# Four alternating attention layers on one core: full layers project queries and keys in five unpadded blocks, and most of the last output projection is moved ahead of the last head group

## The chip, the cores and the metric

The kernel runs on one core of a Trainium2 chip. The metric is device time in microseconds (us) from the first to the last instruction's end on that core. "Granted clock" is the share of full TensorE clock that the hardware allowed, as the profile records it.

## The reference, cut to what matters

```python
def _A_ref(x, wqkv, wo):                      # windowed layer; B is the same without the mask
    B, S, D = x.shape                         # 1, 2048, 640
    H = 32; Dh = D // H; W = 256              # 32 heads of 20
    q, k, v = ...                             # x @ wqkv, split by head
    scores = einsum("bhqd,bhkd->bhqk", q, k) * (Dh ** -0.5)
    mask = (idx[:, None] - idx[None, :] >= 0) & (idx[:, None] - idx[None, :] < W)
    p = softmax(where(mask, scores, -1e9))
    return merge_heads(einsum("bhqk,bhkd->bhqd", p, v)) @ wo

x = A_x
x = x + _A_ref(_layernorm(x), A_wqkv, A_wo)   # layer 0, windowed
x = x + _B_ref(_layernorm(x), B_wqkv, B_wo)   # layer 1, full
x = x + _A_ref(_layernorm(x), A_wqkv, A_wo)   # layer 2, windowed
x = x + _B_ref(_layernorm(x), B_wqkv, B_wo)   # layer 3, full
```

All data are bf16. A head has 20 elements.

## The kernel before

The kernel splits the 2048 tokens into 4 chunks of 512 and the 32 heads into 8 groups of 4. A *unit* is one chunk of queries of one group of heads in one layer. Its scores come out transposed (keys on the 128 partitions, 512 queries along the free axis), three banks of PSUM at a time: three score matmuls, one exponential of 128x1536 on ScalarE. This is a *tile*. Two tiles of PSUM alternate. Value matmuls follow two or three tiles later.

The four heads of a group lie in four strips of 32 partitions. A head has 20 elements, and in this kernel the other 12 rows of each strip hold zeros, because the projection weights are padded with zero columns. The score matmul reads the whole strip, 32 rows:

```python
def k(self, kc, j):
    ...
    return t[32 * j : 32 * j + 32, o * P : (o + 1) * P]
def q(self, j, q0, qn):
    ...
    return t[32 * j : 32 * j + 32, q0 * P : (q0 + qn) * P]
```

Full layers project each group of each chunk (eight groups, five matmuls of 512 columns each, for queries and for keys), store the padded result to HBM and load it back one unit at a time:

```python
def t_full(l, n, c, g):                       # n: 0 queries, 1 keys; 8 groups g
    while "prep_b" not in ready: yield ("wait", 1)
    ...
    wt = yield from take_w(l, n, c, g)
    yield from project(wt, xnT[l, c], staged) # five matmuls, then an eviction
    dst = k_d[l][:, g, c * C : (c + 1) * C] if n else q_d[l][:, c, g, :]
    nc.sync.dma_start(out=dst, in_=staging.pop())
```

Projections, values and output projections are generators that a scheduler steps while it emits tiles. A step ("hold", cost) keeps the same task running; a step ("pe", cost) lets another one come next:

```python
def project(wt, xt, dst):
    mb = yield from take_m()
    pq = ps[:, mb, :]
    for dc in range(KD):                      # KD = 5
        nc.tensor.matmul(pq, lhsT=wt[:, dc, :], rhs=xt[:, dc, :],
                         start=(dc == 0), stop=(dc == KD - 1))
        if dc < KD - 1:
            yield ("hold", 0.22)
    evac(dst(), pq)
    drop_m(mb)
    yield ("pe", 0.22)
```

The very last output projection (8 blocks of 128x320, each a sum over 8 head groups) runs when the last head group has been normalised, so all 64 matmuls and 8 additions stand after the last exponential.

The softmax here doesn't subtract the row's maximum and nothing guards it: scores larger than these inputs give would overflow.

## Time and profile before

| | before |
|---|---|
| time, median of 4 fast runs of the comparison | 2517.38 us (2514.48 to 2525.18) |
| profiled execution | 2509.4 us, mean granted clock 0.762 |
| exponentials | 1695, the same in every kernel here |
| projection matmuls of queries and keys | 1280 |
| TensorE busy / ScalarE busy | 81% / 90% |

The prediction shows most lines of this profile. One that it does not show is the granted clock in the 40 equal slices of the span (a digit is tenths of full speed), from the page of the kernel before:

```profile
PEclk9899899887866798958888589769865575557555
```

Read it from left to right: nearly full clock in layer 0, some 0.8 through the long mixed stretch, and about 0.55 in the last quarter, where only full attention is left.

### The profile page before, as it was taken

What the parts mean: (1) busy time and instruction counts of PE and PEld (TensorE: products, weight loads), DVE (VectorE), ACT (ScalarE), POOL (GpSimd) and SP (SyncE); (2) the same over time, 40 slices, a digit from 0 to 9 for tenths busy, and PEclk for the clock granted to TensorE, in tenths of its full rate; (3) what the DMA queues carried; (4) which work ended last, traced back from release to release, by engine and by line L of the source; (5) the groups of instructions that cost most, each with busy time, mean ns of one, the idle gap of its engine ahead of it and who ended that gap; (6) DMA issues with size and microseconds to landing.
All of it is one profiled execution on the core that took longest, in us unless ns stands there. A gap on an engine that the chain in (4) does not pass through costs nothing.

```text
span 2509.4 us, 37786 instructions
## 1 busy us (share of the span) xinstructions
PE 2037.4 (81%) x15424; PEld 729.9 (29%) x15424; DVE 868.8 (35%) x1956; ACT 2251.3 (90%) x1812; POOL 48.4 (2%) x129
## 2 busy tenths in 40 slices
PE   6889798788887888778887889788877777777777
PEld 3344233222322233223322233232222222222222
DVE  6787575222242334343335334542210010001001
ACT  6778687799989998999989988899999999999995
POOL 2000000000000000000000000000000000000000
PEclk9899899887866798958888589769865575557555
DMA  4221322421210123112222034013211010011000
GB/s 156 79 69 50 110 82 80 124 89 64 67 54 17 48 60 117 45 33 59 65 74 71 1 96 123 25 34 93 85 39 48 33 43 33 33 41 51 33 17 11
DMA packets 114637, 153.70 MB, mean 61 GB/s; under 512 B 11296, under 2 KB 97824, under 8 KB 114464
## 3 DMA queue, kind: packets, MB, share of 16 engines
q1 hardware_dynamic: 114464, 151.30, 19.9%
q8 instruction: 120, 1.97, 0.3%
q14 instruction: 53, 0.43, 0.1%
HBM read 121.11 MB, written 30.15 MB: 60 GB/s over the span
## 4 chain that ended last, share of the span: by engine, by line
ACT 44%; PE 30%; issue 15%; DVE 9%; DMA 2%; SPq 0%; POOL 0%; ACTq 0%; DVEq 0%; POOLq 0%
ACT pt L834 43%; PE ps L318 10%; PE ps L820 7%; PE ps L874 4%; PE ps L484 4%; PE ps L405 3%; DVE pt L859 3%; DMA wqk<-wqk_d 1%; DVE st L269 1%; PE ps L369 1%; DVE oT L682 1%; PE ps L728 1%; DVE x_sb L492 1%; DVE qa L269 0%; DVE on L732 0%
## 5 line engine op out<-in xcount | busy, mean ns | idle before, releaser
L834 ACT ACTIVATE pt<-ps 128x1536 bf16<-128x1536 f32 (+2 forms) x1695 | 2196.4, 1513 | 191.7 <-PE ps L820 167.7
L820 PE MATMUL ps<-qt,kt 32*128 32x512 bf16 x4096 | 695.4, 491 | 313.8 <-ACT pt L834 296.4
L874 PE MATMUL ps<-pt,vt 128*21 128x512 bf16 x4096 | 518.4, 493 | 10.9 <-DVE oT L680 4.2
L820 PEld LDWEIGHTS <-kt 32*128 32x128 bf16 x4096 | 202.3, 95 | 761.7 <-issue 744.0
L318 PE MATMUL ps<-xnT,wqk 128*128 128x512 bf16 x1280 | 369.5, 427 | 31.6 <-DMA wqk<-wqk_d 19.4
L859 DVE TENSOR_TENSOR pt<-pt,masks 128x1024 bf16<-128x1024 bf16 (+6 forms) x403 | 239.0, 625 | 148.7 <-ACT pt L834 148.4
L682 DVE CAST oT<-ps 128x512 bf16<-128x512 f32 x112 | 76.7, 685 | 451.1 <-PE ps L874 450.8
L874 PEld LDWEIGHTS <-vt 128*21 128x21 bf16 x4096 | 106.1, 91 | 327.0 <-issue 322.0
L484 PE MATMUL ps<-wop,on 128*128 128x320 bf16 x1024 | 180.3, 325 | 8.9 <-DVE x_sb L492 6.3
L318 PEld LDWEIGHTS <-wqk 128*128 128x128 bf16 x1280 | 118.2, 105 | 211.7 <-issue 110.4
L269 DVE CAST st<-ps 128x512 bf16<-128x512 f32 x124 | 85.7, 691 | 232.6 <-PE ps L318 228.3
L820 PE MATMUL ps<-qa,ka 32*128 32x384 bf16 (+2 forms) x1408 | 130.6, 312 | 34.7 <-ACT pt L834 32.1
L492 DVE TENSOR_TENSOR x_sb<-x_sb,ps 128x320 bf16<-128x320 bf16 x128 | 62.0, 485 | 223.6 <-PE ps L484 223.3
L405 PE MATMUL ps<-wv,xnT 128*128 128x320 bf16 x640 | 114.3, 317 | 8.2 <-DVE vs L269 2.3
L484 PEld LDWEIGHTS <-on 128*128 128x128 bf16 x1024 | 97.8, 104 | 78.3 <-issue 38.4
L732 DVE TENSOR_TENSOR on<-oT,ps 128x512 bf16<-128x512 bf16 x128 | 87.6, 684 | 92.7 <-PE ps L728 89.6
L874 PE MATMUL ps<-pt,va 128*21 128x384 bf16 (+2 forms) x1408 | 87.9, 319 | 15.7 <-DVE oT L682 15.4
L709 DVE RECIPROCAL rz<-ps 128x16 f32<-128x16 f32 x128 | 32.8, 256 | 144.6 <-PE ps L704 132.1
L820 PEld LDWEIGHTS <-ka 32*128 32x128 bf16 x1408 | 40.1, 95 | 114.4 <-issue 108.7
L405 PEld LDWEIGHTS <-xnT 128*128 128x128 bf16 x640 | 58.3, 101 | 51.6 <-issue 30.0
L728 PE MATMUL ps<-rT,spread 32*128 32x128 bf16 x512 | 64.6, 262 | 4.8 <-DVE rT L721 3.8
L728 PEld LDWEIGHTS <-spread 32*128 32x128 bf16 x512 | 46.7, 113 | 26.9 <-issue 21.4
(50 smaller groups left out, 640.9 us busy)
## 6 DMA issues: line engine op xcount, KB each, us to landing
wqk<-wqk_d SPq DMA_DIRECT2D x240, 160.0 KB
kt<-k_d SPq DMA_DIRECT2D x48, 512.0 KB
vt<-v_d SPq DMA_DIRECT2D x48, 336.0 KB
qt<-q_d SPq DMA_DIRECT2D x80, 128.0 KB
k_d<-st SPq DMA_DIRECT2D x64, 128.0 KB
q_d<-st SPq DMA_DIRECT2D x64, 128.0 KB
v_d<-vs SPq DMA_DIRECT2D x16, 336.0 KB
wqk_d<-wqk SPq DMA_DIRECT2D x32, 160.0 KB
```

The source lines that it names most:

```text
L269: nc.vector.tensor_copy(out=out_, in_=in_)
L318: nc.tensor.matmul(pq, lhsT=wt[:, dc, :], rhs=xt[:, dc, :], start=(dc == 0), stop=(dc == KD - 1),)
L405: nc.tensor.matmul(pv, lhsT=xt[:, dc, i * P : (i + 1) * P], rhs=wv_sb[l % 2][:, dc, h * HD : (h + 1) * HD], start=(dc == 0), stop=(dc == K ...
L484: nc.tensor.matmul(yp, lhsT=on[:, g, qb * P : (qb + 1) * P], rhs=wop[:, g, i * HD : (i + 1) * HD], start=(g == 0), stop=(g == G - 1),)
L492: nc.vector.tensor_tensor(out=xv, in0=xv, in1=yp, op=ALU.add)
L682: nc.vector.tensor_copy(out=oT[:], in_=op)
L728: nc.tensor.matmul(zb[:, qb * P : (qb + 1) * P], lhsT=spread4[:, qb, :], rhs=rT[:], start=True, stop=True,)
L732: nc.vector.tensor_tensor(out=on[:, g, :], in0=oT[:], in1=zb, op=ALU.mult)
L820: nc.tensor.matmul(sp[:, i, col * P : (col + qn) * P], lhsT=u.k(kc, j), rhs=u.q(j, q0, qn), start=True, stop=True,)
L834: nc.scalar.activation(out=pt[:, i:k, b0 * P :], in_=sp[:, i:k, b0 * P :], func=ACT.Exp, scale=SCALE,)
L859: nc.vector.tensor_tensor(out=pt_[:, i:k, b0 * P :], in0=pt_[:, i:k, b0 * P :], in1=mv_, op=ALU.mult,)
L874: nc.tensor.matmul(op[32 * j : 32 * j + VW, q0 * P : (q0 + qn) * P], lhsT=u.v(kc, j), rhs=pt[:, i, col * P : (col + qn) * P], start=(first ...
```

## The change

The intent is less TensorE work and fewer stalls. A full layer's 640 columns are projected as five dense blocks of 128 instead of eight padded ones, so 240 of 1280 matmuls go. What is stored to HBM has no padding; four small loads put each head's 20 rows into its strip. The 12 rows below stay unwritten, so the score matmuls of full layers must read 20 rows (`self.rows`). The weights need no preparation in padded form, and a prefetched one is awaited for four tiles. The first full unit moves one windowed unit later. The first queries and keys come ahead of the values, constants are made earlier, and seven eighths of the last output projection are accumulated ahead.

```diff
-    k_d = {l: dram.tile([P, G, S], ...) for l in (1, 3)}
-    q_d = {l: dram.tile([P, NC, G, C], ...) for l in (1, 3)}
+    k_d = {l: dram.tile([D, S], ...) for l in (1, 3)}
+    q_d = {l: dram.tile([NC, D, C], ...) for l in (1, 3)}
 ...
+        wtick[l, n, c, i] = state["tick"] + 4
+        if l % 2:
+            a = n * D + i * P
+            nc.sync.dma_start(out=t[:], in_=wq_view[1][:, :, a : a + P])
+            return t
 ...
+        while state["tick"] < wtick[key]:
+            yield ("wait", 1)
 ...
-    def t_full(l, n, c, g):
-        while "prep_b" not in ready:
-            yield ("wait", 1)
+    def t_full(l, n, c, b):
 ...
-        dst = k_d[l][:, g, c * C : (c + 1) * C] if n else q_d[l][:, c, g, :]
+        rows = slice(b * P, (b + 1) * P)
+        dst = k_d[l][rows, c * C : (c + 1) * C] if n else q_d[l][c, rows, :]
 ... (t_out: last projection split into t_before_last and one matmul per block)
+            self.rows = 32 if self.windowed else DH
 ...
-            return t[32 * j : 32 * j + 32, o * P : (o + 1) * P]
+            return t[32 * j : 32 * j + self.rows, o * P : (o + 1) * P]
 ... (the same for q)
-        nc.sync.dma_start(out=kt[key][:, k0 * P : k1 * P], in_=k_d[l][:, g, k0 * P : k1 * P])
-        nc.sync.dma_start(out=qt[key][:], in_=q_d[l][:, c, g, :])
+        for j in range(4):
+            rows = slice((4 * g + j) * DH, (4 * g + j + 1) * DH)
+            strip = slice(32 * j, 32 * j + DH)
+            nc.sync.dma_start(out=qt[key][strip, :], in_=q_d[l][c, rows, :])
+            cols = slice(k0 * P, k1 * P)
+            nc.sync.dma_start(out=kt[key][strip, cols], in_=k_d[l][rows, cols])
 ... (t_prep_b removed; order of units, of the first tasks and of the constants)
```

## The prediction

> **What bounds the kernel now.** I read the page's busy shares first, then the chain that ended last, then ScalarE's waits, and then a table of busy time by stretch, because the average mixes stretches with different limits.
>
> The busy shares and the chain from the page of the kernel before (engine, busy us, share of the span, number of instructions; then shares of the chain):
>
> ```profile
> PE 2037.4 (81%) x15424; PEld 729.9 (29%) x15424; DVE 868.8 (35%) x1956; ACT 2251.3 (90%) x1812; POOL 48.4 (2%) x129
> ...
> ACT 44%; PE 30%; issue 15%; DVE 9%; DMA 2%; SPq 0%; POOL 0%; ACTq 0%; DVEq 0%; POOLq 0%
> ```
>
> ScalarE (ACT) is busy 2251 of 2509 us, and 2196 us of that are the exponentials of L834. The change touches none of these. So the most that any schedule can give is ScalarE's idle time, 258 us, and the question is how much of it goes. Next, what ScalarE waits for (total us, times, longest):
>
> ```profile
> ACT pt L834 <- PE ps L820: 167.7, 180, 15.0
> ...
> ACT xnT L267 <- PE ps L369: 14.9, 3, 14.1
> ```
>
> It waits for score matmuls (L820) that come late, and once for the first transposes. The stretches say where (start:end, length, then busy us and instruction count of PE, PEld, DVE, ACT, POOL, then granted clock, DMA share, GB/s):
>
> ```profile
> 252.00:316.00 64.00, 50.45 (x411) 18.76 (x410) 34.65 (x73) 39.72 (x35) 0.38 (x1) 0.89 0.37 111
> ...
> 420.00:480.00 60.00, 45.91 (x303) 16.94 (x302) 19.87 (x36) 37.08 (x32) 2.19 (x5) 0.86 0.41 117
> 480.00:560.00 80.00, 63.48 (x453) 20.92 (x449) 20.54 (x45) 74.95 (x56) 0.00 (x0) 0.85 0.33 99
> 560.00:620.00 60.00, 49.98 (x348) 17.27 (x344) 15.04 (x35) 56.06 (x43) 0.00 (x0) 0.75 0.21 69
> 620.00:1815.00 1195.00, 988.56 (x7709) 361.36 (x7707) 458.82 (x1002) 1095.63 (x828) 14.59 (x40) 0.80 0.21 61
> 1815.00:2484.00 669.00, 518.93 (x3341) 150.33 (x3341) 60.36 (x158) 666.39 (x497) 0.00 (x0) 0.57 0.11 35
> 2484.00:2509.00 25.00, 15.20 (x76) 8.26 (x75) 6.10 (x14) 0.23 (x1) 0.00 (x0) 0.70 0.07 26
> ```
>
> ScalarE's idle time is length less ACT busy. 1815 to 2484 has under 3 us of it: that stretch is bound by ScalarE and nothing but a faster exponential helps. The idle time lies in the start (19 us before 28 us; from the timeline the first exponential starts at 28.02), in layer 0 from 28 to 252 (42 us), in the entry to the first full layer from 252 to 480 (about 59 us), in 480 to 620 (9 us), in the mixed stretch to 1815 (99 us), and in the end (25 us). In the entry it is a few long stalls, not a rate. From ScalarE's timeline (start, us, operation, idle before it and its releaser):
>
> ```profile
> 271.46 2.37 ACT L834 ACTIVATE pt<-ps 128x1536 bf16<-128x1536 f32 x2 [14.98 <-PE ps L820]
> ...
> 430.14 2.37 ACT L834 ACTIVATE pt<-ps 128x1536 bf16<-128x1536 f32 x2 [7.19 <-PE ps L820]
> ...
> 472.18 2.37 ACT L834 ACTIVATE pt<-ps 128x1024 bf16<-128x1024 f32 x2 [7.09 <-PE ps L820]
> ```
>
> With two of 2.5 us beside them these five are 34 us. TensorE's own waits just before are DMAs: 2.75 us for projection weights, then 5.80 us for the query tile loaded back from HBM (at 262 and 270 us), 6.05 and 5.25 us for weights (427 and 468 us).
>
> **What the Trainium skill says.** (1) "TensorE: Matmul & The Clock Gate", section "What's actually happening": the array runs at half rate until it has been busy for a window. The trace agrees: five 512-column projections take 1.25 us in dense stretches and 2.31 us after the DMA waits, and ScalarE's late stretch has a granted clock of 0.57. (2) "SBUF — State Buffer", section "Who interferes with whom": VectorE copies in a two-port mode and GpSimd exclude each other for a whole instruction. The trace agrees: the first normalised tile (VectorE, L360) is on the chain for 5.59 us from 9.82 us, where its mean is 0.53 us, while GpSimd clears the output weights (4.36 us) and the masks (1.38 us). (3) "DMA: Bandwidth & Descriptors", section "Why a DMA increments its semaphore by 16 and not by 1": the engines of a transfer are the largest number up to 16 that divides its outer dimension, so a strip of 20 rows would use 10. No load of keys before has 20 rows, so the trace cannot tell. (4) Same page, "Specifications": under 512 bytes per descriptor the rate falls. The new weight loads have pieces of 256 bytes; no such load is in this trace.
>
> **The change part by part.**
>
> *Projections.* Per full layer, 4 chunks, 2 kinds, 8 groups of 5 matmuls become 5 blocks of 5: over two layers 640 become 400. So 240 of 1280 matmuls of this row go:
>
> ```profile
> L318 PE MATMUL ps<-xnT,wqk 128*128 128x512 bf16 x1280 | 369.5, 427 | 31.6 <-DMA wqk<-wqk_d 19.4
> ```
>
> The mean of 427 ns overlaps its neighbours; 369.5 / 1280 = 0.289 us is what one occupies. 240 x 0.289 = 69 us of PE, and 48 evictions (0.69 us each on VectorE, not the bound). The two instruction orders, aligned by score matmuls, say where: against before, 10 more come ahead of the first full score matmul (units moved), 45 go from the first 256 of these (entry), 85 from the next 256 (480 to about 610 us), 120 from the mixed stretch.
> - 480 to 620: ScalarE idles 9 us and most of the extra work leaves: **5 us**.
> - Mixed stretch: its extra PE work is 640 projections x 0.289 = 185, 280 of values x 0.18 = 50, 576 of output x 0.176 = 101, together 336 us. 120 x 0.289 = 35 us is a tenth; a tenth of 99 us idle is 10, the whole 35 is the ceiling. I choose **13 us**, as the tight places (1380 to 1760, 33 us idle) lose 85 of the 120.
> - Entry: 45 fewer at some 0.25 us is 11 us, partly under the stalls: **4 us**.
>
> *Loads and their order.* The first full unit moves one windowed unit later. A trace of the scheduler's decisions while building shows that before, its last keys are projected, stored and loaded back at the very tile that uses them (all forced at tile 120); after, the projections start at tile 117, the load is issued at 123, and use is at 124. That is four to six tiles at 1.2 us against a store and load of 2 to 3 us each: most of 15 us goes. Every weight is now awaited four tiles after its issue, also if prefetched, which should remove the 7 us waits. The second preparation of weights (1.6 MB in, 2.5 MB written) goes. Of 34 us of stalls I count **24 us** saved, leaving some for eight small loads per unit.
>
> *Costs.* The same waiting makes five more windowed units of layer 0 start with forced projections (tiles 100 to 120), each exposing an eviction of 0.6 to 0.7 us: **minus 4 us**.
>
> *Start.* The clearing of the output weights goes to VectorE before x lands, and the masks are made early, so the 5.6 us copy should be 0.5; the constants may delay the statistics by 1 us: 4 us. The first query and key group comes before the 40 value matmuls (6.32 us), worth 0 where PE is the limit and 6 where ScalarE is: **6 us** together.
>
> *End.* After the last scale at 2488.67 us the 64 output matmuls and 8 adds last until 2506.69: 18 us. Afterwards 8 matmuls and 8 adds of 0.49 us remain, about 4.3 us. The other 56 go into tiles of the last unit, seven per tile: 1.1 us on top of two bursts of 0.33 us at full clock is 1.76 us in a tile of 1.34 us, so 8 x 0.42 and some for the slow clock, 4 us, come back. Net **9.7 us**.
>
> Sum: 5 + 13 + 4 + 24 - 4 + 6 + 9.7 = 57.7 us. 2520.2 - 57.7 = 2462.5.
>
> **The rivals.** *Hidden behind ScalarE*: exponentials are the same 1695, so shorter PE work only lengthens PE's idle time; only the end, the 15 us stall and a little of the start count, about 28 us, 2492 us. For it: 1815 to 2484. Against it: 99 us idle in the mixed stretch, with PE as releaser. *Small transfers take over*: the loads of queries and keys go from 160 to 640 issues on one queue, each 0.32 to 0.43 us, so a unit's nine issues take 3.8 us where three took 1.2, and 256-byte pieces may land late. In the entry, with 8 units, that could give back 15 us: 2478 us. Against it: loads are issued several tiles ahead, and bytes of keys stored fall by 3/8. *The clock falls*: a less busy PE is granted half clock more often (0.57 in the late stretch), and the remaining bursts cost twice; this could eat the 13 us of the mixed stretch: 2475 us.
>
> **Range and chances.** All favourable (stalls gone wholly, start 11, mixed 25) gives about 2432; the hidden case with a little loss gives 2497. 2% faster is 2469.8, 8 us above my estimate, so I give faster 0.6. All parts but one save, so slower by 2% is 0.02.
>
> **What would show it.** Right: 15184 PE matmuls, 1040 projections, ACT busy within 10 us of 2251; first exponential near 18 to 22 us; no ScalarE wait above 6 us between 250 and 480; the last exponential followed by 12 us, not 25; idle in the mixed stretch about 86. Wrong: a long wait on kt, qt or the weight loads, granted clock lower in the mixed stretch with the same ScalarE idle there, or stalls over 5 us in the last 20 us of the exponentials.

## The result, and the profile after

The changed kernel took **2533.61 us** (median of 4 fast runs, 2531.3 to 2537.18) against 2517.38 us before: a ratio of 1.0061, with a 95% interval of 1.0033 to 1.0089. A ratio here is the mean time of one kernel's fast runs over the mean of the other's fast runs of the same rounds, so it is not quite the ratio of the two medians. This is a small loss, and 2533.61 lies well outside the range of 2432 to 2497.

First the page of the changed kernel: busy shares, the granted clock by slice, the shares of the chain that ended last, then the groups of the full layers' scores and of the projections (busy us, mean ns of one, idle before them). Below it, for comparison, the scores' group in the kernel before.

```profile
PE 2082.1 (82%) x15089; PEld 725.8 (29%) x15184; DVE 832.7 (33%) x1895; ACT 2259.8 (89%) x1819; POOL 38.8 (2%) x112
...
PEclk9889997756765679657886579668565555557556
...
ACT 43%; PE 28%; issue 13%; DVE 5%; DMA 0%; SPq 0%; POOL 0%; ACTq 0%; DVEq 0%
...
L848 PE MATMUL ps<-qt,kt 20*128 20x512 bf16 x4096 | 737.7, 520 | 300.0 <-ACT pt L862 288.0
L323 PE MATMUL ps<-xnT,wqk 128*128 128x512 bf16 x945 | 303.6, 444 | 30.2 <-issue 9.7
```

```profile
L820 PE MATMUL ps<-qt,kt 32*128 32x512 bf16 x4096 | 695.4, 491 | 313.8 <-ACT pt L834 296.4 <-DMA qt<-q_d 5.8
```

240 matmuls are gone (15184 weight loads where there were 15424; 95 matmul records are missing from this trace), yet TensorE was busy for 2082 us instead of 2037. It is each matmul that became longer: a projection went from 427 to 444 ns. The scores, which lost 12 of 32 rows, went from 491 to 520 ns and from 695 to 738 us in all. The mean granted clock fell from 0.762 to 0.701, and of the 24 slices from the seventh to the thirtieth 15 have a lower digit than before and one a higher. ScalarE's busy time is the same within 9 us. DMA has left the chain (2% to 0%).

The stretches of the changed kernel (start:end, length, busy us and count of PE, PEld, DVE, ACT, POOL, granted clock, DMA share, GB/s):

```profile
252.00:316.00 64.00, 55.36 (x483) 22.24 (x489) 39.70 (x82) 47.45 (x46) 0.38 (x1) 0.97 0.36 99
...
420.00:480.00 60.00, 52.04 (x344) 20.87 (x344) 22.45 (x50) 44.13 (x38) 1.82 (x4) 0.81 0.29 71
480.00:560.00 80.00, 64.32 (x398) 18.46 (x399) 13.13 (x32) 75.39 (x57) 0.00 (x0) 0.59 0.16 45
560.00:620.00 60.00, 50.54 (x333) 16.28 (x332) 11.91 (x33) 58.46 (x45) 0.00 (x0) 0.58 0.14 39
620.00:1840.00 1220.00, 1016.26 (x7517) 356.97 (x7564) 441.47 (x977) 1094.60 (x825) 14.61 (x40) 0.72 0.19 47
1840.00:2510.00 670.00, 530.06 (x3335) 154.21 (x3335) 62.76 (x163) 657.76 (x490) 0.00 (x0) 0.55 0.09 27
2510.00:2535.00 25.00, 14.62 (x106) 5.87 (x104) 7.42 (x18) 13.56 (x10) 0.00 (x0) 0.74 0.08 27
```

ScalarE idles less in 252 to 316 (17 instead of 24 us) and from 480 to 620 (6 instead of 9). In the mixed stretch it idles 125 us instead of 99, at a granted clock of 0.72 instead of 0.80. In the late stretch it idles 12 us where it had under 3.

The waits of ScalarE after (total us, times, longest), and from its timeline the two longest stalls on late scores (start, us, operation, idle before it):

```profile
ACT pt L862 <- PE ps L848: 189.2, 222, 4.6
ACT xnT L267 <- PE ps L374: 15.7, 3, 12.2
```

```profile
269.70 2.37 ACT L862 ACTIVATE pt<-ps 128x1024 bf16<-128x1024 f32 x2 [4.15 <-PE ps L848]
...
388.03 8.36 ACT L862 ACTIVATE pt<-ps 128x1024 bf16<-128x1024 f32 x7 [4.57 <-PE ps L848]
```

So the long stalls that the change aimed at are gone (longest 4.6 instead of 15.0 us; one more of 5.1 us, at 478 us, has no releaser in the profile), and still the total grew, 180 waits of 167.7 us to 222 of 189.2 us: many small delays took the place of few large ones.

At the start, a detail of the changed kernel's timeline (all engines):

```profile
10.48 1.01 POOL L288 MEMSET wqk<- 128x240 bf16 x4
...
10.76 3.03 DVE L365 TENSOR_SCALAR xn<-x_sb,rstd,nmr 128x640 bf16<-128x640 bf16 x2
...
11.68 1.58 POOL L288 MEMSET wqk<- 128x240 bf16 x5
```

Two normalised tiles took 3.03 us, not 0.5 each, while GpSimd was clearing the pad columns of the weights: the lock that the prediction cites from "SBUF — State Buffer" has not gone. It has a new partner on GpSimd (the clearing of the weights, not of the output weights and masks) and holds for less than the 5.59 us of one tile before. The first exponential still came at 21.89 us.

The end of the changed kernel (timeline of TensorE and VectorE after the last scale):

```profile
2529.07 2.31 PE L491 MATMUL ps<-wop,on 128*128 128x320 bf16 x8 [0.78 <-DVE on L773]
2529.56 3.27 DVE L500 TENSOR_TENSOR x_sb<-raw_o,ps 128x320 bf16<-128x320 f32 x8 [0.54 <-PE ps L491]
```

Eight matmuls and eight additions in 3.8 us, where before it took 18 us.

To compare kernels whose times drift apart, I align them by the number of the exponential: all have the same 1695 in the same number, so the time from the n-th to the m-th is the time of (nearly) the same work. This table is worked out from the traces; each cell is us and granted clock. The rows of 0 to 25 and 25 to 100 move by 2 to 5 us between runs of the same code (the first two columns, which are the same there).

```
exponentials     before      end only (b_end)   changed     changed, 32 rows (a_rows32)
start to first    28.0          28.1             21.9         21.8
0-25           29.9 0.94     32.2 0.84        41.1 0.88    40.6 0.87
25-100        129.9 0.91    134.8 0.87       133.3 0.87   135.2 0.87
100-125        50.6 1.00     50.6 1.00        58.7 0.97    57.5 1.00
125-150        54.7 0.88     55.4 0.88        47.7 0.96    47.5 0.96
150-240       121.1 1.00    123.4 0.97       121.4 0.90   121.0 0.91
240-300        99.7 0.87     99.9 0.87        96.8 0.76    93.0 0.81
300-360        87.6 0.79     87.6 0.79        80.3 0.50    80.3 0.50
360-1200     1214.6 0.80   1218.5 0.79      1243.3 0.72  1214.1 0.76
1200-1400     270.1          270.1            278.0        271.4
1400-1694     396.1          399.9            400.6        401.3
to the end        27.1          12.4             12.3         12.3
sum              2509.4        2513.1           2535.5       2496.2
```

Most of the loss stands in one row, 360 to 1200: the mixed stretch, 28.7 us longer than before. 1200 to 1400 adds 7.9 us. The end saved 15 us, as intended, of which 4 or so return in the last tiles before it.

### The profile page after: what moved, and what is told of

Same layout as the page of the kernel before. It is cut to its first block, busy times and chain, and to the rows that moved or that the text cites.

```text
span 2535.5 us, 37399 instructions
## 1 busy us (share of the span) xinstructions
PE 2082.1 (82%) x15089; PEld 725.8 (29%) x15184; DVE 832.7 (33%) x1895; ACT 2259.8 (89%) x1819; POOL 38.8 (2%) x112
## 4 chain that ended last, share of the span: by engine, by line
ACT 43%; PE 28%; issue 13%; DVE 5%; DMA 0%; SPq 0%; POOL 0%; ACTq 0%; DVEq 0%
ACT pt L862 43%; PE ps L323 7%; PE ps L848 7%; PE ps L905 5%; PE ps L491 4%; PE ps L410 3%; DVE pt L887 2%; PE ps L374 1%; PE ps L769 1%; DVE st L269 1%; DVE oT L723 0%; DVE qa L269 0%; PE ps L522 0%; DVE ka L269 0%; DVE x_sb L500 0%
## 5 line engine op out<-in xcount | busy, mean ns | idle before, releaser
L862 ACT ACTIVATE pt<-ps 128x1536 bf16<-128x1536 f32 (+2 forms) x1695 | 2201.4, 1528 | 211.8 <-PE ps L848 189.2
L848 PE MATMUL ps<-qt,kt 20*128 20x512 bf16 x4096 | 737.7, 520 | 300.0 <-ACT pt L862 288.0
L905 PE MATMUL ps<-pt,vt 128*21 128x512 bf16 x4096 | 550.9, 524 | 10.3 <-DVE oT L723 5.4
L848 PEld LDWEIGHTS <-kt 20*128 20x128 bf16 x4096 | 205.4, 96 | 782.0 <-issue 767.1
L323 PE MATMUL ps<-xnT,wqk 128*128 128x512 bf16 x945 | 303.6, 444 | 30.2 <-issue 9.7
L887 DVE TENSOR_TENSOR pt<-pt,masks 128x1024 bf16<-128x1024 bf16 (+5 forms) x404 | 240.0, 623 | 217.8 <-ACT pt L862 217.4
L848 PE MATMUL ps<-qa,ka 32*128 32x384 bf16 (+2 forms) x1408 | 140.3, 328 | 37.6 <-ACT pt L862 32.1
L323 PEld LDWEIGHTS <-wqk 128*128 128x128 bf16 x1040 | 100.4, 108 | 172.3 <-issue 108.0
L410 PE MATMUL ps<-wv,xnT 128*128 128x320 bf16 x640 | 120.3, 328 | 7.7 <-ACT xnT L267 2.1
L269 DVE CAST st<-ps 128x512 bf16<-128x512 f32 x76 | 52.5, 690 | 127.2 <-PE ps L323 124.4
```

The source lines that it names most:

```text
L269: nc.vector.tensor_copy(out=out_, in_=in_)
L323: nc.tensor.matmul(pq, lhsT=wt[:, dc, :], rhs=xt[:, dc, :], start=(dc == 0), stop=(dc == KD - 1),)
L410: nc.tensor.matmul(pv, lhsT=xt[:, dc, i * P : (i + 1) * P], rhs=wv_sb[l % 2][:, dc, h * HD : (h + 1) * HD], start=(dc == 0), stop=(dc == K ...
L848: nc.tensor.matmul(sp[:, i, col * P : (col + qn) * P], lhsT=u.k(kc, j), rhs=u.q(j, q0, qn), start=True, stop=True,)
L862: nc.scalar.activation(out=pt[:, i:k, b0 * P :], in_=sp[:, i:k, b0 * P :], func=ACT.Exp, scale=SCALE,)
L887: nc.vector.tensor_tensor(out=pt_[:, i:k, b0 * P :], in0=pt_[:, i:k, b0 * P :], in1=mv_, op=ALU.mult,)
```

## The experiments

Theories. **Rows**: the granted clock depends on how many rows of the array the matmuls use; scores on 20 rows instead of 32 lower it, and the lower clock is the loss. **Fewer projections**: TensorE does less, so its clock is granted less often (the prediction's rival). **Small loads or the new waits**: 640 small loads and the waits on weights hold tiles up. The third is weakened by the profile already: DMA has 0% of the chain, and TensorE's longest wait is 1.2 us on keys or queries and 3.8 us on weights, where before it was 6.7 and 6.3.

All fifteen runs, each with its ratio to the kernel before in the same rounds. All gave correct results but b_rows8.

| run | what it is | median us | before, same rounds | ratio (95%) | granted clock |
|---|---|---|---|---|---|
| b_rows20 | before, scores on 20 rows | 2561.62 | 2523.33 | 1.0154 (1.0134–1.0174) | 0.726 |
| a_rows32 | changed, scores on 32 rows | 2494.37 | 2523.33 | 0.9881 (0.9858–0.9904) | 0.726 |
| b_end | before, new end only | 2510.78 | 2523.33 | 0.9951 (0.9930–0.9972) | 0.757 |
| a_nowait | changed, no wait on prefetched weights | 2545.74 | 2523.33 | 1.0080 (1.0043–1.0116) | 0.700 |
| b_rows8 | before, scores on 8 rows | 2616.41 | 2519.23 | 1.0387 (1.0355–1.0418) | 0.693 |
| b_cols32 | before, values on 32 columns, not 21 | 2517.24 | 2519.23 | 0.9989 (0.9963–1.0015) | 0.756 |
| a_r32_d128 | a_rows32 + needless matmul, 128 columns per tile | 2540.97 | 2519.23 | 1.0083 (1.0051–1.0114) | 0.734 |
| a_r32_d384 | a_rows32 + needless matmul, 384 columns per tile | 2544.93 | 2519.23 | 1.0101 (1.0073–1.0129) | 0.775 |
| a_r32_redo | a_rows32, 240 matmuls put back in bursts of eight | 2542.45 | 2518.82 | 1.0098 (1.0082–1.0114) | 0.734 |
| a_r32_paced | the same, costed for the scheduler | 2539.05 | 2516.53 | 1.0084 (1.0059–1.0109) | 0.745 |
| a_r32_tasks | a_rows32, 240 matmuls put back as tasks of five | 2506.70 | 2517.03 | 0.9951 (0.9934–0.9969) | 0.758 |
| a_r32_vfirst | a_rows32, values ahead of queries and keys | 2486.81 | 2518.82 | 0.9875 (0.9856–0.9893) | 0.729 |
| a_r32_lead3 | vfirst, no wait on prefetched weights in layer 0, first full unit prepared 3 units earlier | 2479.97 | 2518.82 | 0.9846 (0.9828–0.9864) | 0.731 |
| a_r32_lead5 | as lead3, but 5 units earlier, and that unit one later | 2477.08 | 2518.82 | 0.9857 (0.9816–0.9898) | 0.735 |
| lead5_split13 | lead5, tasks that may be interrupted | 2469.24 | 2517.03 | 0.9816 (0.9796–0.9836) | 0.724 |

Between sets of runs the kernel before itself moves from 2516.5 to 2523.3 us, so across sets the ratios are the safer comparison; where the two ways differ I give both.

### 1. Rows alone, in both directions

In the kernel before, the 12 pad rows are zeros, so leaving them out is correct and changes nothing else:

```diff
             self.windowed = l % 2 == 0
+            self.rows = 32 if self.windowed else DH
 ...
-            return t[32 * j : 32 * j + 32, o * P : (o + 1) * P]
+            return t[32 * j : 32 * j + self.rows, o * P : (o + 1) * P]
```

> The kernel before, and in it only the score matmuls of the full layers read 20 partitions of each strip in place of 32; instructions, data, order, loads and result are the same. Theory R (the granted TensorE clock falls because a matmul over fewer rows counts as less activity): 20 to 45 us slower than before (2537 to 2562 us), mean granted clock 0.68 to 0.72 in place of 0.76, and the loss in the stretches where full and other work mix, and where output projections run in the last 670 us. Rival P (the clock falls because 240 projections are gone) and rival L (the eight small loads per unit): no change, 2517 us within 8, clock 0.76.

Measured: 2561.62 us, 1.54% slower than before. The other direction, the change with 32 rows, needs pads that are zero. The tiles that keys and queries are loaded to become fixed buffers, cleared once on VectorE during layer 0:

```diff
-        kt[key] = kvp.tile([P, S], BF16, name="kt", tag="kt")
-        qt[key] = qtp.tile([P, C], BF16, name="qt", tag="qt")
+        kt[key] = kt_all[:, loads[0] % 3, :]
+        qt[key] = qt_all[:, loads[0] % 4, :]
+        loads[0] += 1
 ...
-            self.rows = 32 if self.windowed else DH
+            self.rows = 32
 ...
+            if 30 <= t < 72 and t % 6 == 0:
+                n = (t - 30) // 6
+                z = kt_all[:, n, :] if n < 3 else qt_all[:, n - 3, :]
+                nc.vector.memset(z, 0.0)
```

> The changed kernel with score matmuls over 32 partitions again: keys and queries lie in fixed buffers whose spare rows are cleared once, and the loads still write 20 rows of each strip. Theory R: 2490 to 2508 us (25 to 43 us less than the changed kernel), clock back to 0.75 or more. Rivals P and L: stays at 2533 within 8.

Measured: 2494.37 us, 1.2% faster than before and 39 us (45 by ratios) faster than the change as it was. So 20 rows cost 38 us in the old kernel and about 39 to 45 us in the new one. (The second figure holds the fixed buffers and their clearing too; b_rows20 has nothing of the kind.) The time came as expected, the clock of "0.75 or more" did not: it is 0.726, for the reason that section 5 finds. ScalarE's waits for scores (total us, times, longest) fall from 189.2 us in the changed kernel to:

```profile
ACT pt L870 <- PE ps L856: 154.4, 198, 4.6
```
Without the loss of rows the change would have landed inside the predicted range, at its upper edge. The mean clock is not a measure by itself: b_rows20 and a_rows32 have the same 0.726, and their times are 67 us apart.

To see whether it is a matter of degree, 8 rows (the result is wrong, relative error 0.23):

```diff
+            self.rows = 32 if self.windowed else 8
```

> The kernel before with score matmuls of the full layers over 8 of 32 partitions; wrong result on purpose, the same durations of every instruction at equal clock. If activity is counted by rows, fewer rows still cost more: 2570 to 2620 us and a mean clock below the 0.726 of the run with 20 rows. If only whether a strip is complete matters (20 is not, 32 is), it equals the run with 20 rows, 2555 to 2568.

Measured: 2616.41 us, 3.9% slower. With 20 and 8 rows the kernel takes 1.015 and 1.039 of its time with 32, and the granted clock is 0.726 and 0.693, where it is 0.75 to 0.76 with 32. The mixed stretch shows how. For each kernel one line: start:end, length, busy us and count of PE, PEld, DVE, ACT, POOL, granted clock. The kernel before:

```profile
610.00:1820.00 1210.00, 1001.30 (x7817) 367.15 (x7812) 462.79 (x1012) 1110.46 (x838) 14.59 (x40) 0.80 0.21 61
```

Before with 20 rows (b_rows20):

```profile
611.00:1862.00 1251.00, 1062.78 (x7837) 373.25 (x7834) 464.66 (x1017) 1115.52 (x841) 14.61 (x40) 0.74 0.20 59
```

Before with 8 rows (b_rows8):

```profile
623.00:1910.00 1287.00, 1117.30 (x7836) 379.05 (x7835) 464.85 (x1017) 1119.72 (x842) 14.61 (x40) 0.69 0.19 57
```

The same number of matmuls, within 20, keeps TensorE busy for 1001, 1063 and 1117 us, as the clock goes 0.80, 0.74, 0.69; ScalarE's idle time, length less busy, goes 100, 135 and 167 us. And the change with 20 rows against the change with 32, in that order:

```profile
601.00:1845.00 1244.00, 1037.06 (x7673) 365.51 (x7720) 447.58 (x993) 1117.06 (x842) 14.61 (x40) 0.72 0.18 47
```

```profile
597.00:1811.00 1214.00, 1002.74 (x7717) 361.00 (x7714) 447.82 (x993) 1113.84 (x841) 14.56 (x40) 0.76 0.19 48
```

Idle 127 against 100 us. Is a matmul on 20 rows perhaps itself slower? Three scores at half clock, then three at full clock, a few us on; first before (32 rows), then b_rows20:

```profile
2031.51 0.61 PE L820 MATMUL ps<-qt,kt 32*128 32x512 bf16 x3
...
2034.08 0.39 PE L820 MATMUL ps<-qt,kt 32*128 32x512 bf16 x3
```

```profile
2080.08 0.61 PE L821 MATMUL ps<-qt,kt 20*128 20x512 bf16 x3
...
2082.87 0.39 PE L821 MATMUL ps<-qt,kt 20*128 20x512 bf16 x3
```

0.61 and 0.39 us in both: at the same clock a score costs the same with 20 rows as with 32. Only how often the full clock is granted differs. Nor does a busy TensorE have the full clock by that alone: one stretch of before with nothing but full attention,

```profile
1880.00:2030.00 150.00, 117.27 (x723) 31.38 (x720) 12.52 (x35) 150.00 (x113) 0.00 (x0) 0.50 0.13 41
```

has TensorE busy for 117 of 150 us, no gap between matmuls above 0.73 us, and half clock all the way. (It costs nothing there: ScalarE is busy all of the 150 us.)

The late stretch shows the switching most plainly. At the start of an output projection (full-array matmuls among the scores) the clock rises. The bursts of eight of its matmuls in before, from TensorE's timeline:

```profile
2032.05 2.10 PE L484 MATMUL ps<-wop,on 128*128 128x320 bf16 x8
...
2035.05 1.26 PE L484 MATMUL ps<-wop,on 128*128 128x320 bf16 x8
```

and in the changed kernel:

```profile
2063.00 2.31 PE L491 MATMUL ps<-wop,on 128*128 128x320 bf16 x8
...
2077.96 2.31 PE L491 MATMUL ps<-wop,on 128*128 128x320 bf16 x8
...
2082.75 1.26 PE L491 MATMUL ps<-wop,on 128*128 128x320 bf16 x8
```

Before, the first burst ends at full clock and the second runs at it (1.26 us). After, four bursts run at half clock (2.31 us) before the fifth gets it. That much is chance in part: in the changed kernel's next output projection, and in both of b_rows20, one burst was enough. The steadier difference is how long the full clock stays. The intervals of full clock that the trace records around the two output projections of this stretch, in us:

```
before      27.3 + 3.4                     34.1
a_rows32    30.7                           27.3 + 3.4
changed     13.7                           30.7
b_rows20    13.7 + 3.4 + 3.4               13.7 + 10.2
b_rows8      6.8 + 3.4 + 3.4 + 3.4          6.8 + 3.4
```

In sum these are 65, 61, 44, 44 and 27 us. All are multiples of 3.41 us. This is the window of 3413 ns that the Trainium skill states ("TensorE: Matmul & The Clock Gate", section "What's actually happening"), and the traces agree with it. The page says that the clock is set by how busy the array has been; these runs add that the same matmuls, in the same order, are granted less of it when they use fewer rows. How the hardware counts is not shown.

Do columns count as well? The value matmuls produce 21 columns of a 32-column strip, here widened to 32 with whatever follows in the buffer (their result in the extra rows of PSUM is not used):

```diff
-            return vt[self.l, self.c, self.g][:, o : o + VW]
+            n = 32 if o + 32 <= key_blocks(self.l, self.part)[1] * 4 * VW else VW
+            return vt[self.l, self.c, self.g][:, o : o + n]
 ... (the output of the value matmul widened to match)
```

> The kernel before with the value matmuls of the full layers writing 32 columns of a strip in place of 21 (the further 11 are the next head's values and are multiplied by zero rows later, so the result stays right). If columns count as activity as rows do, the clock rises over 0.76 and the time falls by 10 to 40 us. If only rows count: no change, within 8 us.

Measured: 2517.24 us, ratio 0.9989, with a granted clock of 0.756 in a page of 2516 us: no effect that the runs resolve. The further columns, from 21 to 32, bought no clock here; rows do, and rows of zeros do too, since the pads are zeros in before and in a_rows32.

### 2. The end alone

The kernel before with nothing but the split of the last output projection (the part of the diff named t_before_last):

```diff
+        last = (l, c) == (3, NC - 1)
 ...
-                for g in range(G):
+                for g in range(G - 1 if last else 0, G):
 ...
+        if (l, c, g) == (3, NC - 1, G - 2):
+            push("before_last", t_before_last(), 0, 8.0)
```

> The kernel before with the last output projection mostly ahead, and nothing else of the change. All theories: the end after the last exponential shrinks from 25 to 11 us; some 3 to 5 us come back in the last 20 exponentials. So 8 to 12 us faster than before: 2506 to 2509 us.

Measured: ratio 0.9951, 12.5 us less by medians. In the table above, its last row is 14.7 us shorter than before's, and exponentials 1400 to 1694 are 3.8 us longer: the 14 saved and 4 given back of the prediction.

### 3. The wait on prefetched weights

```diff
             wtiles[order[at]] = get_w(*order[at])
+            wtick[order[at]] = 0
```

> The changed kernel without its new rule that a prefetched weight is awaited four tiles. Scheduling theory S: the six forced projections at tiles 100 to 120 go back to one, so the 8 us lost between exponentials 100 and 125 come back, but the first full unit is forced again at its own tile and up to 10 us of the long stall return: within 10 us of the changed kernel, 2525 to 2540. Theory R: the granted clock stays at 0.70, since rows are as in the changed kernel. If waiting for weights were the main loss, it would fall to 2515 or less.

Measured: 2545.74 us, ratio 1.0080 against the change's own 1.0061: not a gain. By exponentials, 100 to 125 falls from 58.7 back to 50.6 us, so the wait does cost the 8 us of late projections there. But 125 to 150 rises from 47.7 to 56.8 us, because one load is then forced again in that place, and the mixed stretch was 1253.0 us. The time is 6 us above what was expected. The wait moves a cost within the entry; it is not the cause of the loss.

### 4. Raising the clock with needless work

If the clock is what is missing, more array use might pay. In a_rows32, one matmul of 128 rows that writes into the score bank before the first score overwrites it, per tile of the mixed stretch; 128 columns wide, then 384:

```diff
                 sp = ps[:, 0:3, :] if t % 2 == 0 else ps[:, 3:6, :]
+                u0 = cur[0][0]
+                if index[1,0,0,'b'] <= index[u0.l,u0.c,u0.g,u0.part] <= index[3,0,G-1,'b']:
+                    nc.tensor.matmul(sp[:, 0, 0:128], lhsT=ident[:], rhs=masks[:, 0, 0:128],
+                                     start=True, stop=True)
```

> The changed kernel with 32 rows, and one needless full-array matmul of 128 columns ahead of the scores of each tile from the second half of the first full chunk to the end of the mixed stretch (its output is overwritten). If the clock there is what costs time, more activity pays: mean clock in that stretch up from about 0.75, 5 to 25 us less than the 2494 us of the kernel without it. If TensorE's work itself is the limit, some 1000 x 0.06 to 0.11 us come on top: up to 2520 us.

> The same with 384 columns, three times the needless work: clock near 0.9 or more in the stretch if activity governs it. The work is 0.16 us a tile at full clock, 160 us over 1000 tiles, of which ScalarE's pace hides most: 2470 to 2520 us, and the sign is what it tells.

Measured: 2540.97 and 2544.93 us, both far above what was expected. The clock did rise, from 0.726 to 0.734 and 0.775, and the time rose by 47 and 51 us (by ratios 51 and 55). In this place the needless work takes more of TensorE's time than the clock gives back. They stand between the release of a bank and the scores that ScalarE waits for (TensorE idled 114 us before those of 128 columns until ScalarE was done); whether they would pay elsewhere was not tested. The pad rows are different in that they take no time at equal clock.

### 5. What the removed projections are worth

The change lost 240 matmuls; the prediction put 22 us on them. Put back into a_rows32 in the crudest way, every block does three of its five matmuls once more, in one uninterrupted burst of eight (0.22 us below is the scheduler's figure for one):

```diff
-    def project(wt, xt, dst):
+    def project(wt, xt, dst, again=0):
 ...
+        for dc in range(again):
+            nc.tensor.matmul(pq, lhsT=wt[:, dc, :], rhs=xt[:, dc, :],
+                             start=(dc == 0), stop=(dc == again - 1))
 ...
-        yield from project(wt, xnT[l, c], staged)
+        yield from project(wt, xnT[l, c], staged, 3)
```

> The changed kernel with 32 rows, and the 240 removed projection matmuls put back: each of the 80 block projections of a full layer first does three of its matmuls once more, and they are overwritten. Everything else and the result stay. If the removed work was worth what the prediction said for 480 us and after (5 + 13 us), it costs 18 to 25 us: 2512 to 2520. If the clock gives back what the work takes (theory C), under 10 us: 2496 to 2504, with the mean clock up from 0.726 to 0.75.

Measured: 2542.45 us, 48 us more than a_rows32 (55 by ratios). 240 matmuls of 0.22 us are 53 us, so it looks as if all of the work stood on the path. But then before itself, which has these matmuls too, ought to be far slower than it is. Either the work has this price, or it is the length of the burst: eight matmuls in a row are 1.8 us, longer than a tile (1.34 us), five are 1.1. The first attempt to tell them apart let the scheduler account for the extra three:

```diff
+            yield ("hold", 0.22)
 ...
-                    push(("qk"[n], l, c, b), t_full(l, n, c, b), first, 1.1)
+                    push(("qk"[n], l, c, b), t_full(l, n, c, b), first, 1.76)
```

> As the run that puts the 240 projection matmuls back, with one difference: the repeated matmuls go through the scheduler as the others do, one at a time and counted in its estimate of the work left (1.76 in place of 1.1 per block), as the 640 of the kernel before were. Theory T (what a projection costs depends on whether it is paced into TensorE's gaps or comes as a burst): in the mixed stretch the cost falls from 26 us to under 8, total 2500 to 2520. Rival W (each projection matmul on TensorE costs its 0.2 us whatever its place): 2535 to 2545 as with bursts, and the small gain against the kernel before must have another cause.

Measured: 2539.05 us. This was a poor experiment: a task that holds is never interrupted, so the bursts were still of eight, and only the accounts had changed. It settles nothing about bursts, but it takes a rival away: the work was not dear merely because the scheduler had left it out of its accounts. The better control puts the same 240 matmuls back as 48 more tasks of five, each with its weight load, its eviction and its store to memory that nobody reads, 128 tasks as in before:

```diff
-            for b in range(KD):
-                g = b * P // 80
+            for b in (0, 1, 11, 2, 3, 13, 4, 14):
+                g = {11: 2, 13: 5, 14: 7}.get(b, b * P // 80)
 ...
+        if b > 9:
+            dst = spare_d[l, c, n, b][:]
```

> The changed kernel with 32 rows and the 240 projection matmuls put back as 48 further tasks of five matmuls, each with its weight load, eviction and store (to memory that nothing reads), due where the padded groups were due before: the same number of tasks, matmuls and evictions as before. The two earlier put-backs made 80 bursts of eight, since a task once begun is never interrupted. Theory B (length of a burst: five matmuls, 1.25 us, fit beside a 1.34 us tile, eight, 2 us, don't): the mixed stretch costs under 10 us more than without, total 2500 to 2515. Rival W (the work costs its time in any shape): 2530 to 2545.

Measured: 2506.70 us (10 runs, 2492.8 to 2511.08): 12 us more than a_rows32 by medians, 18 by ratios. So the 240 matmuls are worth 12 to 18 us in bursts of five, and some three or four times as much in bursts of eight. By the traces, exponentials 360 to 1200 hold 40 bursts of eight in a_r32_redo, and 128 of five and none longer in a_r32_tasks, as in before. The added tasks also stand in other places and load their own weights, so that the length alone makes the price is likely and not shown. ScalarE's waits for scores say the same (total us, times, longest); first the bursts of eight, then the tasks of five:

```profile
ACT pt L872 <- PE ps L858: 196.2, 233, 5.7
```

```profile
ACT pt L874 <- PE ps L860: 166.6, 216, 5.2
```

That is 42 and 12 us more than in a_rows32. Against a_rows32, 360 to 1200 is 30 us longer in the first (1243.8) and 8 in the second (1222.3), and 300 to 360 is 5 us longer in the second (85.5 against 80.3). This run also shows that the "fewer projections" theory has a grain of truth: with the tasks back, the mean granted clock is 0.758 instead of 0.726, and still the kernel is slower: what the clock gives is less than what the work costs.

### 6. Towards a better version

Four further versions of a_rows32. The table above shows the changed order at the start as no gain: the first exponential is 6 us earlier, but the next 25 take 9 us more than in b_end and 11 more than in before, since the 40 value matmuls then stand among them. So, values first again:

```diff
+        push(("v", l, c), t_v(l, c, (0, 1)), need[0], 5.6)
         for g in range(G):
 ...
-            if g == 0:
-                push(("v", l, c), t_v(l, c, (0, 1)), need[0], 5.6)
 ... (and the first units wait for the values, as before)
```

> The changed kernel with 32 rows, with the values of a windowed chunk projected ahead of its first queries and keys, as before. If TensorE is the limit of the first chunk, the early first exponential is worth nothing: first exponential back at 26 to 28 us, the 25th within 3 us of the other order, total within 6 us of 2494. If the order is worth the 4 to 6 us of the prediction, it is slower by that.

Measured: 2486.81 us, ratio 0.9875 against 0.9881. By medians it is 7.6 us; the ratios are within each other's intervals. The traces have first exponential plus 25 more at 55.3 instead of 62.4 us, which agrees with the medians; but their clocks there, 0.94 and 0.87, differ too, so the gain is likely and not settled.

Then the entry. No wait on prefetched weights in layer 0, and what the first full unit needs is due three, or five, units earlier (in the second, that unit also starts one windowed unit later):

```diff
+            if l == 0:
+                wtick[order[at]] = 0
 ...
-        push(("ln", l, c), t_ln(l, c), need[0], 1.6)
+        push(("ln", l, c), t_ln(l, c), need[0] - 5 * (l == 1 and c < 2), 1.6)
 ... (the same for the values, the first block and the output projection of layer 0)
-        if g in (1, 2, 3, 4, 6):
+        if g in (2, 3, 4, 5, 6):
```

> As the run with values first, and the wait for prefetched weights is left out in layer 0, and normalisation, values and the first key and query block of the first two chunks of layer 1 are due three units earlier, so that the first full unit is loaded four tiles ahead with three forced projections in place of six. If forced work and the late first load are what the entry loses: 5 to 15 us less than 2494. If the entry is bound by TensorE's work: within 5.

> The same with five units of lead and the first full unit one windowed unit later: load twelve tiles ahead of use, three forced projections. Same two outcomes as with three units: 2480 to 2490, or within 5 of 2494.

Measured: 2479.97 and 2477.08 us, ratios 0.9846 and 0.9857. Their medians lie 14 and 17 us under a_rows32's and 7 and 10 under a_r32_vfirst's of the same rounds; but the intervals of the ratios overlap, and one of the four runs of a_r32_lead5 took 2494.0 us, so the gain is likely and not settled. Between the two there is no difference that the runs resolve.

Last, what the burst experiments suggest: after the early part, a scheduler may turn to another task between any two matmuls of a task, and the rate is raised from 1.1 to 1.3.

```diff
+    def go():
+        return "hold" if state["early"] else "pe"
 ...
-                yield ("hold", 0.22)
+                yield (go(), 0.22)
 ...
-            return min(1.1 * r, 0.9)
+            return min(1.3 * r, 0.9)
```

> The fastest version so far (32 rows, five units of lead), with tasks that may be interrupted between two matmuls after the start, and the scheduler's rate raised from 1.1 to 1.3 so that as few projections are forced. Theory B: ScalarE's idle time in the mixed stretch (about 95 us there) falls by 10 to 40 us: 2437 to 2467. Rival: the single free PSUM bank is held longer and the chains of the normalisation wait for it, 2477 to 2500.

Measured: 2469.24 us (2468.99 to 2472.35), ratio 0.9816 (0.9796 to 0.9836). It is the best version, 48 us below before and 64 below the change, though just above the range that I had expected, and "faster by over 2%" stays unclear. Its busy shares, from its page:

```profile
PE 2054.8 (83%) x15184; PEld 703.1 (28%) x15184; DVE 833.1 (34%) x1902; ACT 2257.9 (92%) x1818; POOL 40.8 (2%) x112
```

360 to 1200 took 1199.5 us, against 1212.5 in lead5 and 1214.1 in a_rows32. That is a second sign, and no proof, that it is burst length that ScalarE waits for, though two things (interruption and rate) changed at once, so their shares are open.

## Why the prediction was wrong

**The step that failed** is one that has no line of its own in the prediction. Its sum, "5 + 13 + 4 + 24 - 4 + 6 + 9.7 = 57.7 us", has no term for the score matmuls' going from 32 to 20 rows. So it counted this as free; and at equal clock it is (0.61 and 0.39 us both ways). What it missed is that the granted clock depends on the rows. The missing term measured: 38 us lost when it alone was done to the kernel before, and 39 to 45 us won back when it was undone in the changed kernel. That is the whole loss against before. It is not the whole miss: a_rows32, at 0.9881, gained 29 us where 57.7 were predicted, and the terms below hold the rest.

**"The clock falls"** was named as a rival, with the right symptom ("granted clock lower in the mixed stretch": 0.80 to 0.72) but with a cause that explains only the half of it that did no harm. The prediction wrote that "a less busy PE is granted half clock more often". Fewer projections do lower the clock: from 0.79 (a_r32_tasks) to 0.76 (a_rows32) between exponentials 360 and 1200. But with them gone that stretch is 8 us shorter, as long as in before (1214.1 and 1214.6 us). The further fall to 0.72 comes with the rows, and it is this that costs 29 us there. The prediction gave the rival 13 us to eat; the rows ate three times as much, for they act on the whole stretch and not only on the saved work. Its sign, "the same ScalarE idle there", did not come either: the idle time rose, from 99 to 125 us.

**The end** was right: minus 9.7 predicted, minus 12.5 measured by b_end, with 4 given back in the last tiles as reckoned.

**Projections**: 5 + 13 + 4 predicted; 12 to 18 measured as a whole. By traces, exponentials 300 to 360 (514 to 602 us in before, most of the 480 to 620 us of the prediction) gave 5.2, and the mixed stretch 8 rather than 13. The term was somewhat too large, mainly in the mixed stretch.

**Entry, waits and start** were mis-sized: 24 − 4 + 6 = 26 us predicted. a_r32_tasks has the rows, projections and end of b_end and differs from it in entry, waits and start, and in how queries and keys are stored and loaded; the ratios are equal (0.9951 both), the medians 4 us apart, the traces 6. The stalls did go: 125 to 150 is 7.8 us shorter and 150 to 300 some 7 (a_r32_tasks against b_end). That is 15 of the 24; the prediction took 24 of "34 us of stalls" as removable; why the other 9 did not come was not tested. The late projections at 100 to 125 cost 7 to 8 us where 4 was reckoned, as a_nowait shows by removing them. The first two normalised tiles, reckoned at 0.5 us each, took 3.03 together. And the start is no gain at all: 6 us earlier at the first exponential (21.89, as predicted), but at the 25th 3 us later than b_end and 5 later than before. The prediction valued the new order at "0 where PE is the limit and 6 where ScalarE is" and added 6 for both parts of the start together; that it came to nothing is what TensorE as the limit would give, though no run took the parts apart beyond a_r32_vfirst.

Part of the entry could not be judged from before's one trace: its exponentials 0 to 100 took 159.8 us, and the same code in b_end took 167.0 and in b_rows20 167.3, with a clock of 0.84 instead of 0.94 in the first 25. That is chance, of the size of the terms in question. The whole is a sum of gains and one loss that happen to be near each other, and no sign that the change does little.

**"Small transfers take over"** did not occur: the chain has 0% DMA, and TensorE's waits on keys and queries are of 1.2 us at most.

Of the signs that were promised, the counts (15184, 1040 as built), ScalarE's busy time, the first exponential, no stall above 6 us in the entry and the short end (10.8 us after the last exponential) all came out. The idle time of the mixed stretch did not: 125 us instead of 86. It was this single number, with the clock beside it, that carried the result. (A slip that changes nothing: 2469.8 is 7 us above the estimate, not 8.)

Open are how the hardware weighs rows (12 rows less cost 1.5%, 24 rows less 3.9%), whether rows of other data than zeros count differently, and how much of the gain of lead5_split13 comes from each of its two edits.

## What to carry to other kernels

When a change narrows the rows of matmuls that run for most of a kernel, expect the granted TensorE clock to move even though no duration at equal clock does, and compare the clock by stretch before counting any saving; here, zero rows that fill each strip to 32 cost no time and were worth about 40 us. Do not judge by the mean clock, though: it was 0.726 in a version that gained and in one that lost. Extra matmuls for the clock's sake, put ahead of the scores that the bounding engine waited for, did not pay here with TensorE 80% busy. The same extra work cost three or four times as much in bursts longer than a tile as in shorter ones, so try the shorter ones first. A gain at the first instruction of the bounding engine counts only if it is still there some tiles later, so align two traces by the number of its operations.

## What the Trainium skill lacked or had wrong

- "TensorE: Matmul & The Clock Gate", section "What's actually happening", says that the clock follows how busy the array has been. It lacks that the rows in use weigh: the same scores on 20 and 8 rows of each strip took 1.015 and 1.039 of the time on 32, at granted clocks of 0.76 (32 rows), 0.73 and 0.69, with TensorE busy for longer each time. Rows of zeros count; widening the values from 21 to 32 columns did nothing (ratio 0.9989).
- The same page, section "HAM oscillation — how this bites in real kernels", gives as the rule that TensorE should have no idle gaps above about 3.4 us. That is not enough: 150 us of the kernel before with no gap above 0.73 us and TensorE 78% busy ran wholly at half clock. The section after it, on PSUM queues, tells of short idle times that were enough to lose the clock, and is nearer to this trace.
- The same page, section "Part 3: Packing small matmuls — row/col tiling", and "TensorEngine Tiling (Array Packing)" describe strips of 32 rows without saying what a strip that is not full costs. Here it cost no duration (0.61 and 0.39 us for three scores with 20 or 32 rows) and 1.5% of the kernel.
- No page has the price of a burst beside a rate-limiting engine: the same 240 matmuls cost 12 to 18 us as tasks of five and 48 to 55 us in bursts of eight, beside tiles of 1.34 us; that the length alone makes it is likely and not shown.
